# Narrow transpose of the softmax sums moved ahead of a cast, and the seventh pair's reciprocals sent through DRAM

## The chip, the core and the metric

The kernel runs on one core of a Trainium2 chip. The metric is the device time of one execution in microseconds (us), as the median of a few runs. The engines are TensorE (PE: matmuls and transposes into PSUM; PEld is its weight load), VectorE (DVE), ScalarE (ACT), GpSimd (POOL) and SyncE (SP, which here issues DMAs only). Each engine works through its own instructions in order; semaphores hold an instruction until what it needs from another engine or a DMA is there.

## The reference, cut to what matters

```python
# q, k, v: (2, 8, 768, 64); proj: (64, 6)
q_bucket = sum((q @ proj > 0) * powers); k_bucket = sum((k @ proj > 0) * powers)
scores = where(q_bucket == k_bucket, q @ k.T / 8, -1e9)
scores = scores - max(scores)
attn = exp(scores)
attn = attn / (sum(attn) + 1e-9)          # the row sums and their reciprocals
x = (attn @ v), heads side by side        # (1536, 512)
x = maximum(x @ w_in, 0) ** 2 @ w_out     # first MoE block, 512 -> 2048 -> 512
h = x @ w_in2
out = (h * sigmoid(h)) @ w_out2           # second MoE block
```

## The kernel before

There are 16 heads of 768 rows, worked off as 8 pairs of heads (`p` = 0 to 7). A pair has four units `u` (two heads, two halves of 384 query rows each), so there are 32 units, and each unit has six key tiles of 128. After attention the two MoE blocks follow in one long stretch whose order a planner sets (class `Plan`); the change does not touch it.

Attention is one hand-written loop over steps `d` (L1258). A step handles two key tiles, `g = 2d` and `g+1`. On PE a step is: six transposes of exponentials into two PSUM banks of the pool `ps_t` (`transp`, L1025, three per bank), four products of values with tiles that are two steps old (`av`, L1049 and L1050), and four score matmuls for a later tile (`score_mm`, L989). Every product is made of a high and a low part: ScalarE casts each transposed bank to the high part `th` (`t_hi`, L1030), and VectorE subtracts it from the bank to get the low part `tl` (`t_lo`, L1036). VectorE also takes the row maximum (L996), and ScalarE the exponential (`score_exp`, L1009), which adds up the row sums into `sums[p]`. A finished unit is copied by ScalarE (`ob`, L1060), and two DMAs on SP's queue move its two halves to `ta` and `tb`; POOL adds them up (`x_sum`, L1103). There are two `ta` buffers and one `tb`.

In the steps 5, 17, 29, 41, 53, 65 and 77 (here: **long steps**) PE also forms the hash bits of the next pair by twelve matmuls (`bits_mm`, L789), which VectorE compares (`bits_cmp`, L795, two of them). Two DMAs on SP's queue (`place_bits`, L919) put the bit rows into the `qq` and `kk` tiles, which the score matmuls read two steps later. VectorE has some word operations of the MoE weights in these steps too (L958, L962, L966).

The sums of pair `p` become reciprocals at step `d0+2`, where `d0 = 12(p+1)` (`norm_rows`, L1071). They must be laid out along the columns of `x`. This is done in three ways:

- Pairs 0 to 5, at the long steps 17 to 77: a **narrow transpose** on PE (`row_turn`, L1077: 128 sums x 12 into 12 rows at the end of the bank of tile `g+1`), a copy by ScalarE (L1079), a DMA into a DRAM scratch (`row_put`, L1083), and two DMAs back that repeat each row over 64 partitions (`row_get`, L1088). Then POOL multiplies `x` by it (`x_mul`, L1115) and splits blocks for the MoE (`x_put`, L1124 and L1125).
- Pair 6: POOL spreads the reciprocals (L1074), PE transposes them with six 128x128 transposes at step 93 (`rb_mm`, L1097) into a bank pair of `ps_s`, ScalarE copies the result (`x_norm`, L1108), and POOL multiplies.
- Pair 7: POOL spreads them too; after the loop PE transposes them (L1315) and VectorE multiplies (L1317).

What an engine does in a step stands in the order in which the Python calls it. `at(d, f, ...)` puts a call into the list `todo` of a step, run at its end. The narrow transpose stands behind `t_hi(g+1)`:

```python
                transp(g + 1)
                t_hi(g + 1)
                if d in turn:
                    row_turn(turn[d], PT[g + 1][0])
```

Of the kernel before, what the change touches and what calls it, by code (L numbers as in the profile page):

```python
# [11 lines left out]
F32 = mybir.dt.float32  # L12
# [5 lines left out]
ALU = mybir.AluOpType  # L18
# [6 lines left out]
NPAIR = B * H // 2  # L25
NU = NPAIR * 4
QW = 384
# [672 lines left out]
def lsh_attention_moe_moe(ctx, tc, kd, qk, qf, fq, v, pc, wi1, wo1, wi2, wo2, out):  # L700
    nc = tc.nc
# [19 lines left out]
    ps_s = att.enter_context(tc.tile_pool(name="ps_s", bufs=2, space=PSUM))  # L721
# [3 lines left out]
    ident = ac.tile([128, 128], F32, name="ident")  # L725
# [30 lines left out]
    def scale_q(p):  # L756
        q = pair[p]["r"][0]
        nc.scalar.mul(out=q, in_=q, mul=SCALE)
# [217 lines left out]
    P, stats, otile, sums = {}, {}, {}, {}  # L976

    def warm_up(n):
        for _ in range(n):
            mm(warm, zb[:, 0:128], zb[:, 0:512], start=True, stop=True)  # L980
# [13 lines left out]
    def row_max(u, j, s):  # L994
        m = mt[:, (u * 3 + j) % 4]
        nc.vector.tensor_reduce(out=m[:, 0:1], in_=s[:, :, 0:QW], op=ALU.max, axis=AX.XY, negate=True)  # L996
        return m

    def row_live(m):
        nc.vector.tensor_scalar(out=m[:, 1:2], in0=m[:, 0:1], scalar1=LIM, scalar2=1.0, op0=ALU.is_lt, op1=ALU.mult)  # L1000
        nc.vector.tensor_scalar(out=m[:, 2:3], in0=m[:, 0:1], scalar1=LIM, scalar2=m[:, 0:1], op0=ALU.is_lt, op1=ALU.mult)  # L1001

    def score_exp(u, j, s, m):
        p = u // 4
        if u % 4 == 0 and j == 0:
            sums[p] = a2.tile([128, 12], F32, tag="sums", name=f"sums{p}")
        e = P[u, j] = ac.tile([128, S], F32, tag="P", bufs=6, name=f"P{u}_{j}")
        c = (u % 4) * 3 + j
        nc.scalar.activation(  # L1009
            out=e.rearrange("p (a b) -> p a b", a=2),  # L1010
            in_=s[:, :, 0:QW],
            func=AF.Exp,
            scale=m[:, 1:2],
            bias=m[:, 2:3],
            accum_out=sums[p][:, c : c + 1],
        )

    PT = {}

    def transp(g, t=None):  # L1020
        u, kt = divmod(g, KT)
        if t is None:
            t = ps_t.tile([128, 512], F32, tag="t", name=f"t{g}")
        for j in range(3):
            nc.tensor.transpose(t[:, j * 128 : (j + 1) * 128], P[u, j][:, kt * 128 : (kt + 1) * 128], ident)  # L1025
        PT[g] = (t,)

    def t_hi(g):
        th = a1.tile([128, QW], F32R, tag="th", bufs=6, name=f"th{g}")
        nc.scalar.copy(out=th, in_=PT[g][0][:, 0:QW])  # L1030
        PT[g] += (th,)

    def t_lo(g):
        t, th = PT[g]
        tl = a1.tile([128, QW], F32R, tag="tl", bufs=6, name=f"tl{g}")
        nc.vector.tensor_tensor(out=tl, in0=t[:, 0:QW], in1=th.bitcast(F32), op=ALU.subtract)  # L1036
        PT[g] = th, tl

    xs = {}
# [29 lines left out]
    def norm_rows(p):  # L1069
        ri = sums[p]  # L1070
        nc.vector.reciprocal(out=ri, in_=ri)  # L1071
        if p >= NPAIR - 2:
            w = rows[p] = a1.tile([128, 6, 2, 64], F32, tag="rw", bufs=2, name=f"rw{p}")
            nc.gpsimd.tensor_copy(out=w, in_=ri.rearrange("p (h c) -> p c h", h=2).unsqueeze(3).broadcast_to([128, 6, 2, 64]))  # L1074

    def row_turn(p, t):
        nc.tensor.transpose(t[0:12, QW:512], sums[p], ident)  # L1077
        r = turned[p] = a1.tile([12, 128], F32, tag="rt", name=f"rt{p}")
        nc.scalar.copy(out=r, in_=t[0:12, QW:512])  # L1079

# [9 lines left out]
    turned, scratch = {}, {}  # L1090
    rows = {}

    def rb_mm(p):
        s = ps_s.tile([128, 2, 512], F32, tag="s", name=f"rb{p}")
        for c in range(6):
            o = s[:, c // 3, c % 3 * 128 : c % 3 * 128 + 128]
            nc.tensor.transpose(o, rows[p][:, c].rearrange("p h d -> p (h d)"), ident)  # L1097
        return s

    def x_sum(p):  # L1100
        ta, tb = xs[p]
        for r, z in ((slice(0, 64), slice(QW, S)), (slice(0, 128), slice(0, QW))) if p == NPAIR - 1 else ((slice(0, 128), slice(0, S)),):
            nc.gpsimd.tensor_tensor(out=ta[r, z], in0=ta[r, z], in1=tb[r, z], op=ALU.add)  # L1103

    def x_norm(s, p):
        ta = xs[p][0].rearrange("p (a b) -> p a b", a=2)
        if p < NPAIR - 1:
            nc.scalar.copy(out=rows[p].rearrange("p c h d -> p (c h d)").rearrange("p (a b) -> p a b", a=2), in_=s[:, :, 0:QW])  # L1108
        else:
            nc.vector.tensor_tensor(out=x_rows(p).rearrange("p (a b) -> p a b", a=2), in0=s[:, :, 0:QW], in1=ta, op=ALU.mult)  # L1110

    def x_mul(p):
        if p < NPAIR - 1:
# [3 lines left out]
    def x_rows(p):  # L1117
        return yf[:, p % 4, p // 4 * S : p // 4 * S + S]
# [11 lines left out]
        nc.gpsimd.tensor_tensor(out=o, in0=o, in1=b, op=ALU.subtract if MINUS[0].get(k) else ALU.add)  # L1130

    todo = defaultdict(list)
    extra = defaultdict(list)
    mid = defaultdict(list)
    long, scale, turn = {}, {}, {}
    last = defaultdict(list)

    def at(g, fn, *a):
        todo[g].append((fn, a))

    for p in range(1, NPAIR):
        d0 = 12 * (p - 1)
# [18 lines left out]
    for p in range(NPAIR):  # L1161
        d0 = 12 * (p + 1)
        at(d0 + (-3 if p < NPAIR - 1 else -4), norm_sums, p)
        at(d0 + (2 if p < NPAIR - 1 else -3), norm_rows, p)
        at(d0 + (3 if p < NPAIR - 1 else 0), x_sum, p)
        if p == NPAIR - 2:
            extra[d0 + 9].append((rb_mm, x_norm, p))
            at(d0 + 10, x_mul, p)
            at(d0 + 10, x_put, p)
        elif p < NPAIR - 2:  # L1170
            k = d0 + 5
            turn[k] = p
            at(k, row_put, p)
            at(k + 3, row_get, p)
            at(k + 5, x_mul, p)
            at(k + 5, x_put, p)

    for k, d in enumerate(X_STEPS):
        at(d, x_form, k)
    for i, (d_load, d_abs, *d_dve) in enumerate(W_STEPS):  # L1180
# [6 lines left out]
        d0 = d_dve[2]  # L1187
# [6 lines left out]
    with tc.manual_schedule():  # L1194
# [15 lines left out]
        c, k = slice(64, 64 + NBR), first["c"]  # L1210
        nc.vector.tensor_tensor(
            out=pdx, in0=k[:, 0:NBR].unsqueeze(1).broadcast_to([128, 2, NBR]), in1=k[:, NBR : 3 * NBR].rearrange("p (a b) -> p a b", a=2), op=ALU.mult
# [45 lines left out]
        for d in range(-5, G // 2 + 3):  # L1258
            ready, new = new, None
            g = 2 * d  # L1260
            if ready:
                m = row_max(*ready)
            if 0 <= g - 1 < G and g - 1 not in early_lo:
                t_lo(g - 1)
            if ready:
                row_live(m)
            for fn, a in mid.pop(d, []):
                fn(*a)
            if 0 <= g < G and d in (92, 94):
                t = ps_s.tile([128, 2, 512], F32, tag="s", name=f"t{g}")  # L1270
                for i in range(2):
                    transp(g + i, t[:, i])
                t_hi(g)
                t_hi(g + 1)
                t_lo(g)
            elif 0 <= g < G:
                transp(g)
                t_hi(g)
                t_lo(g)
                transp(g + 1)  # L1280
                t_hi(g + 1)
                if d in turn:
                    row_turn(turn[d], PT[g + 1][0])
            more = extra.pop(d, [])
            if ready and more and d not in long:
                score_exp(*ready, m)
            if d in long:
                score_exp(*ready, m)
                if d in scale:
                    scale_q(scale.pop(d))  # L1290
            for n in (g - V_LAG, g + 1 - V_LAG):
                if 0 <= n < G:
                    av(n)
            if d in long:
                t = bits_mm(long[d])
            held = [(dve, pe(p), p) for pe, dve, p in more]
            if d in long:
                bits_cmp(t, long[d], 0)
                t_lo(g + 1)
                bits_cmp(t, long[d], 1)  # L1300
            for dve, t, p in held:
                dve(t, p)
            if ready and not more and d not in long:
                score_exp(*ready, m)
            u, j = divmod(d + 5, 3)
            if u < NU:
                new = u, j, score_mm(u, j)
            for fn, a in todo.pop(d, []) + last.pop(d, []):
                fn(*a)
            warm_up(WARM.get(d, 0))  # L1310
        p = NPAIR - 1
        for z in (1, 0):
            t = ps_t.tile([128, 512], F32, tag="t", name=f"rb{p}_{z}")
            for j in range(3):
                nc.tensor.transpose(t[:, j * 128 : (j + 1) * 128], rows[p][:, 3 * z + j].rearrange("p h d -> p (h d)"), ident)  # L1315
            ta = xs[p][0][:, z * QW : (z + 1) * QW]
            nc.vector.tensor_tensor(out=x_rows(p)[:, z * QW : (z + 1) * QW], in0=t[:, 0:QW], in1=ta, op=ALU.mult)  # L1317
        assert not new
        assert not todo and not extra and not mid and not scale
        att.close()  # L1320


# [3 lines left out]
        t = dict(yf=yf, xk=xk, wpa=wpa, raw=raws, wt=wt, pair=both, src=((wi1, wo1), (wi2, wo2)), out=out)  # L1326
# [58 lines left out]
```

## Time and profile before

| | us |
|---|---|
| median of 3 runs | 729.46 (729.27 to 729.68) |
| profiled execution | 728.33 |
| its span (first to last instruction) | 726.6 |
| PE busy | 714.7 (98%) |
| DVE busy | 610.8 (84%) |
| ACT busy | 539.7 (74%) |
| POOL busy | 258.7 (36%) |

All times below are us from the start of the span. Attention takes the first 235 us or so, the MoE blocks the rest. A timeline row gives the start, the duration, the engine, the line, what is written from what, how often, and in brackets how long the engine was idle before and what ended that. Neighbouring instructions overlap in the pipeline, so a duration is longer than the distance to the next start. The chain of waits follows the work that ended last back to the start and says on which engine each piece of the span was.

### The profile page before, as it was taken

What the parts mean: (1) busy time and instruction counts of PE and PEld (TensorE: products, weight loads), DVE (VectorE), ACT (ScalarE), POOL (GpSimd) and SP (SyncE); (2) the same over time, 40 slices, a digit from 0 to 9 for tenths busy, and PEclk for the clock granted to TensorE, in tenths of its full rate; (3) what the DMA queues carried; (4) which work ended last, traced back from release to release, by engine and by line L of the source; (5) the groups of instructions that cost most, each with busy time, mean ns of one, the idle gap of its engine ahead of it and who ended that gap; (6) DMA issues with size and microseconds to landing.
All of it is one profiled execution on the core that took longest, in us unless ns stands there. A gap on an engine that the chain in (4) does not pass through costs nothing.

```text
span 726.6 us, 10910 instructions
## 1 busy us (share of the span) xinstructions
PE 714.7 (98%) x3643; PEld 612.2 (84%) x3643; DVE 610.8 (84%) x1106; ACT 539.7 (74%) x1012; POOL 258.7 (36%) x242
## 2 busy tenths in 40 slices
PE   8999999999999999999999999999999999999998
PEld 4999898898899888888888888888788888888886
DVE  7999999999998979786797879989778778888840
ACT  6998898898798898486459568878766945854861
POOL 7634755656547512041231223234203110212300
PEclk9999999999999999999999999999999999999999
DMA  5887698697662536124534653368231332345432
GB/s 172 202 199 169 158 204 187 153 222 175 147 157 55 122 107 169 59 73 102 130 88 116 133 134 96 87 143 172 70 124 58 88 89 80 107 102 116 102 110 93
DMA packets 38640, 92.16 MB, mean 127 GB/s; under 512 B 5564, under 2 KB 10524, under 8 KB 38584
## 3 DMA queue, kind: packets, MB, share of 16 engines
q1 hardware_dynamic: 26120, 67.18, 31.7%
q0 software_dynamic: 12032, 23.79, 18.3%
q8 instruction: 29, 0.48, 0.3%
q10 hardware_dynamic: 432, 0.49, 0.2%
q14 instruction: 27, 0.22, 0.1%
HBM read 51.96 MB, written 3.18 MB: 76 GB/s over the span
## 4 chain that ended last, share of the span: by engine, by line
PE 80%; DVE 15%; ACT 3%; issue 1%; DMA 0%; POOL 0%; ACTq 0%; DVEq 0%; POOLq 0%
PE bank L558 36%; PE bank L443 24%; DVE mt L996 7%; PE bank L420 7%; DVE tl L1036 6%; PE s L989 3%; PE t L1025 3%; PE o L1049 2%; PE o L1050 2%; ACT P L1009 2%; PE bs L789 1%; PE bt L789 1%; DVE mt L1001 1%; ACT th L1030 1%; DVE mt L1000 1%
## 5 line engine op out<-in xcount | busy, mean ns | idle before, releaser
L558 PE MATMUL bank<-woh,cell 128*128 128x512 f32 (+1 forms) x392 | 120.0, 385 | 0.0
L558 PE MATMUL bank<-cell,woh 128*128 128x512 f32 x384 | 118.3, 389 | 0.0
L1036 DVE TENSOR_TENSOR tl<-t,th 128x384 fp32r<-128x384 f32 x192 | 104.7, 548 | 0.8 <-ACT th L1030 0.8
L1009 ACT ACTIVATE P<-s,mt 128x768 f32<-128x768 f32 x96 | 95.3, 993 | 11.2 <-DVE mt L1001 8.1
L996 DVE TENSOR_REDUCE mt<-s 128x1 f32<-128x768 f32 x96 | 91.5, 953 | 3.5 <-PE s L989 3.1
L1030 ACT CAST th<-t 128x384 fp32r<-128x384 f32 x192 | 81.9, 483 | 12.5 <-PE t L1025 12.1
L558 PEld LDWEIGHTS bank<-woh,cell 128*128 128x128 f32 x392 | 73.1, 188 | 14.7
L558 PEld LDWEIGHTS bank<-cell,woh 128*128 128x128 f32 x384 | 72.1, 188 | 15.2
L989 PE MATMUL s<-kk,qq 76*128 76x384 f32 (+1 forms) x384 | 83.8, 339 | 0.5 <-ACT P L1009 0.4
L1025 PE MATMUL t<-ident,P 128*128 128x128 f32 x576 | 78.9, 272 | 0.0
L278 DVE TENSOR_TENSOR cell<-bank,cell 128x512 f32<-128x512 f32 x91 | 62.1, 692 | 18.3 <-PE bank L443 13.9
L443 PE MATMUL bank<-xw,wpb 128*128 128x512 f32 x312 | 75.9, 389 | 0.0
L558 PE MATMUL bank<-wol,cell 128*128 128x512 f32 (+1 forms) x196 | 75.4, 385 | 0.0
L558 PE MATMUL bank<-cell,wol 128*128 128x512 f32 x192 | 74.7, 389 | 0.0
L1049 PE MATMUL o<-th,vv 128*128 128x384 f32 x192 | 72.5, 377 | 0.0
L1025 PEld LDWEIGHTS t<-ident,P 128*128 128x128 f32 x576 | 67.8, 140 | 4.5 <-DVE tl L1036 0.2
L989 PEld LDWEIGHTS s<-kk,qq 76*128 76x128 f32 (+1 forms) x384 | 68.3, 188 | 2.6 <-ACT P L1009 1.6
L443 PEld LDWEIGHTS bank<-xw,wpb 128*128 128x128 f32 x312 | 58.5, 188 | 12.4 <-DVE bank L278 0.3
L1050 PE MATMUL o<-tl,vv 128*128 128x384 f32 x192 | 64.3, 335 | 0.0
L588 ACT COPY yf<-bank 128x512 f32<-128x512 f32 x48 | 27.9, 586 | 35.4 <-PE bank L558 34.7
L450 ACT COPY cell<-bank 128x512 f32<-128x512 f32 x39 | 22.9, 587 | 40.7 <-PE bank L443 38.7
L268 ACT CAST cell<-cell 128x512 fp32r<-128x512 f32 x81 | 48.8, 617 | 1.9 <-DMA cell<-cell 0.8
(201 smaller groups left out, 1484.8 us busy)
## 6 DMA issues: line engine op xcount, KB each, us to landing
raw<-in_dram SPq DMA_DIRECT2D x64, 512.0 KB
cell<-cell POOLq DMA_DIRECT2D x23, 256.0 KB, 3.4
qq<-hq SPq DMA_DIRECT2D x28, 192.0 KB
kk<-in_dram POOLq DMA_DIRECT2D x14, 384.0 KB, 5.3
yf<-cell POOLq DMA_DIRECT2D x21, 256.0 KB, 3.3
vr<-in_dram SPq DMA_DIRECT2D x8, 384.0 KB
ta<-ob SPq DMA_DIRECT2D x31, 96.0 KB
tb<-ob SPq DMA_DIRECT2D x31, 96.0 KB
```

What stands on the lines that cost most here:

```text
L278: add("DVE", 0.70, lambda: vec.tensor_tensor(out=val(out), in0=bank[b], in1=val(other), op=ALU.add), [("bank", b), *reads], writes)
L420: mm(bank[b], wpa[n][:, p, 4 * h + j], x[:, q], start=j == 0 and z == 0, stop=j == 3 and z == 2)
L443: mm(bank[b], w[:, p], x[:, q], start=not started and z == 0, stop=z == 2, skip_group_check=started)
L558: mm(bank[b][:, 0:wd], x, y, start=start and i == 0 and z == 0, stop=i == (FB if half is None else 2 * half + 2) - 1 and z == 2, skip_grou ...
L989: mm(s[:, n, 0:QW], t["qq"][h][0:kk, ab, c0 : c0 + 128], t["kk"][h][0:kk, ab, n * QW : (n + 1) * QW], start=ab == 0, stop=ab == 1)
L996: nc.vector.tensor_reduce(out=m[:, 0:1], in_=s[:, :, 0:QW], op=ALU.max, axis=AX.XY, negate=True)
L1009: nc.scalar.activation(out=e.rearrange("p (a b) -> p a b", a=2), in_=s[:, :, 0:QW], func=AF.Exp, scale=m[:, 1:2], bias=m[:, 2:3], accum_ou ...
L1025: nc.tensor.transpose(t[:, j * 128 : (j + 1) * 128], P[u, j][:, kt * 128 : (kt + 1) * 128], ident)
L1030: nc.scalar.copy(out=th, in_=PT[g][0][:, 0:QW])
L1036: nc.vector.tensor_tensor(out=tl, in0=t[:, 0:QW], in1=th.bitcast(F32), op=ALU.subtract)
L1049: mm(o[:, 0:QW], vv, th, start=kt == 0, stop=False)
L1050: mm(o[:, 0:QW], vv, tl, start=False, stop=kt == KT - 1)
```

## The change

The narrow transpose is issued by PE right behind the transposes of tile `g+1`, ahead of ScalarE's cast of that bank; ScalarE's copy of the 12 rows stays behind the cast. Pair 6 takes the way of pairs 0 to 5: narrow transpose at step 88 (not a long step), `row_put` at 88, `row_get` at 90, `x_mul` at 93; its spread on POOL, the six transposes on PE and the 768-column copy on ScalarE go. For pairs 0 to 4 `x_mul` moves from `d0+10` to `d0+13` and `x_put` to `d0+14`. Pair 5 keeps its steps.

```diff
-        if p >= NPAIR - 2:
+        if p == NPAIR - 1:
             w = rows[p] = a1.tile([128, 6, 2, 64], F32, tag="rw", bufs=2, name=f"rw{p}")
...
-    def row_turn(p, t):
-        nc.tensor.transpose(t[0:12, QW:512], sums[p], ident)
+    def row_copy(p, t):
         r = turned[p] = a1.tile([12, 128], F32, tag="rt", name=f"rt{p}")
         nc.scalar.copy(out=r, in_=t[0:12, QW:512])
...
-        if p == NPAIR - 2:
-            extra[d0 + 9].append((rb_mm, x_norm, p))
-            at(d0 + 10, x_mul, p)
-            at(d0 + 10, x_put, p)
-        elif p < NPAIR - 2:
-            k = d0 + 5
+        if p < NPAIR - 1:
+            k = d0 + (5 if p < NPAIR - 2 else 4)
             turn[k] = p
             at(k, row_put, p)
-            at(k + 3, row_get, p)
-            at(k + 5, x_mul, p)
-            at(k + 5, x_put, p)
+            at(k + (3 if p < NPAIR - 2 else 2), row_get, p)
+            x = k + (8 if p < NPAIR - 3 else 5)
+            at(x, x_mul, p)
+            at(x + 1 if p < NPAIR - 3 else x, x_put, p)
...
                 transp(g + 1)
+                if d in turn:
+                    nc.tensor.transpose(PT[g + 1][0][0:12, QW:512], sums[turn[d]], ident)
                 t_hi(g + 1)
                 if d in turn:
-                    row_turn(turn[d], PT[g + 1][0])
+                    row_copy(turn[d], PT[g + 1][0])
```

On PE the order of the instructions around a narrow transpose is the same in both kernels; what each waits for is not. These are PE's rows of step 17 before (`t_885` is the bank of tile `g+1`, `sums` the reciprocals, `o` the output bank that the products with `th` and `tl` open; in brackets the engines whose semaphore an instruction waits for):

```order
L1025 MATMUL t_885<-ident,P_0_689 128x128 [waits DVE_49]
L1025 MATMUL t_885<-ident,P_1_723 128x128
L1025 MATMUL t_885<-ident,P_2_757 128x128
L1077 MATMUL t_885<-ident,sums_191 12x128 [waits Activation_49,Pool_49]
L1049 MATMUL o_897<-th_812,vv_479 128x384
L1050 MATMUL o_897<-tl_814,vv_479 128x384
```

The narrow transpose waits for ScalarE there. The same rows of the changed kernel:

```order
L1025 MATMUL t_885<-ident,P_0_689 128x128 [waits DVE_49]
L1025 MATMUL t_885<-ident,P_1_723 128x128
L1025 MATMUL t_885<-ident,P_2_757 128x128
L1263 MATMUL t_885<-ident,sums_191 12x128 [waits Pool_49]
L1049 MATMUL o_897<-th_812,vv_479 128x384 [waits Activation_49]
L1050 MATMUL o_897<-tl_814,vv_479 128x384
```

The wait for ScalarE now stands one instruction later, on the first product that opens a new output bank.

POOL's rows around the multiplication of pair 1 before (`lp` is the low part of the keys of a later pair, `kk` its key load, `rw` the reciprocals from DRAM):

```order
L754 CAST hk_930<-rk_698 128x768
L1115 TENSOR_TENSOR yf<-rw_1046,ta_415 128x768
L1124 CAST xk<-yf 128x512
L1125 TENSOR_TENSOR xk<-yf,xk 128x512
L774 TENSOR_TENSOR lp_1006<-rk_698,hk_930 128x768
L764 DMA kk_0_1218<-in_dram 64x2x768
L1103 TENSOR_TENSOR ta_857<-ta_857,tb_858 128x768
```

And in the changed kernel:

```order
L754 CAST hk_930<-rk_698 128x768
L774 TENSOR_TENSOR lp_1006<-rk_698,hk_930 128x768
L764 DMA kk_0_1215<-in_dram 64x2x768
L1100 TENSOR_TENSOR yf<-rw_1046,ta_415 128x768
L1109 CAST xk<-yf 128x512
L1110 TENSOR_TENSOR xk<-yf,xk 128x512
L1095 TENSOR_TENSOR ta_857<-ta_857,tb_858 128x768
```

The three instructions that wait for the reciprocals now stand behind the split of the keys and the key load, still ahead of `x_sum`.

POOL's rows at the end of attention before, from pair 6's spread on (`rw_3505` and `sums_2845` are pair 6's, `rw_3719` and `sums_3288` pair 7's; `ta_3122` is pair 6's `x`, `ta_3562` pair 7's):

```order
L1074 COPY rw_3505<-sums_2845 128x768
L1103 TENSOR_TENSOR ta_3122<-ta_3122,tb_3123 128x768
L1130 TENSOR_TENSOR yf<-yf 128x512 x2
L1067 TENSOR_SCALAR sums_3288<-sums_3288 128x2x2
L1067 TENSOR_SCALAR sums_3288<-sums_3288 128x2x4
L1074 COPY rw_3719<-sums_3288 128x768
L1115 TENSOR_TENSOR yf<-rw_3505,ta_3122 128x768
L1103 TENSOR_TENSOR ta_3562<-ta_3562,tb_3563 64x384
```

In the changed kernel (`rw_3640` is what comes back from DRAM for pair 6, `rw_3718` pair 7's spread):

```order
L1095 TENSOR_TENSOR ta_3122<-ta_3122,tb_3123 128x768
L1115 TENSOR_TENSOR yf<-yf 128x512 x2
L1067 TENSOR_SCALAR sums_3288<-sums_3288 128x2x2
L1067 TENSOR_SCALAR sums_3288<-sums_3288 128x2x4
L1100 TENSOR_TENSOR yf<-rw_3640,ta_3122 128x768
L1074 COPY rw_3718<-sums_3288 128x768
L1095 TENSOR_TENSOR ta_3563<-ta_3563,tb_3564 64x384
```

Pair 6's multiplication now stands ahead of pair 7's spread and not behind it, and it waits for a DMA. On SP's queue pair 6's three new DMAs stand behind the first `ta` and `tb` transfers of pair 7.

## Rows read from the trace of the kernel before

**Rows 1.** Busy time of the engines, and the chain's share by engine.

```profile
PE 714.7 (98%) x3643; PEld 612.2 (84%) x3643; DVE 610.8 (84%) x1106; ACT 539.7 (74%) x1012; POOL 258.7 (36%) x242
PE 80%; DVE 15%; ACT 3%; issue 1%; DMA 0%; POOL 0%; ACTq 0%; DVEq 0%; POOLq 0%
```

**Rows 2.** Timeline of PE in step 5, a long step without a narrow transpose.

```profile
25.86 0.82 PE L1025 MATMUL t<-ident,P 128*128 128x128 f32 x6
26.44 0.42 PE L1049 MATMUL o<-th,vv 128*128 128x384 f32 x1
```

**Rows 3.** Timeline of PE in step 17 and the scores two steps later.

```profile
52.64 0.82 PE L1025 MATMUL t<-ident,P 128*128 128x128 f32 x6
54.50 0.27 PE L1077 MATMUL t<-ident,sums 128*12 128x128 f32 x1 [1.04 <-ACT th L1030]
54.53 0.42 PE L1049 MATMUL o<-th,vv 128*128 128x384 f32 x1
...
61.54 0.87 PE L989 MATMUL s<-kk,qq 128*128 128x384 f32 x4
```

**Rows 4.** Timeline of ScalarE in step 17.

```profile
53.50 0.86 ACT L1030 CAST th<-t 128x384 fp32r<-128x384 f32 x2
...
54.97 0.98 ACT L1009 ACTIVATE P<-s,mt 128x768 f32<-128x768 f32 x1
```

**Rows 5.** Groups by line: busy us, mean ns of one, idle before and its releaser.

```profile
L1077 PE MATMUL t<-ident,sums 128*12 128x128 f32 x6 | 1.6, 269 | 6.2 <-ACT th L1030 6.2
L795 DVE TENSOR_SCALAR bt<-bs,tmt 48x384 fp32r<-48x384 f32 x7 | 4.7, 667 | 4.0 <-PE bs L789 4.0
L1115 POOL TENSOR_TENSOR yf<-rw,ta 128x768 f32<-128x768 f32 x7 | 12.9, 1842 | 41.2 <-DMA rw<-rows 41.2
```

**Rows 6.** Timeline of VectorE in steps 17 to 19.

```profile
54.82 0.69 DVE L962 SCALAR_TENSOR_TENSOR wi<-raw,wi 128x512 uint32<-128x512 uint32 x1
...
56.56 0.67 DVE L795 TENSOR_SCALAR bt<-bs,tmt 48x384 fp32r<-48x384 f32 x1 [0.58 <-PE bs L789]
...
57.61 0.66 DVE L795 TENSOR_SCALAR bt<-bt,tmt 48x384 fp32r<-48x384 f32 x1
...
60.38 0.96 DVE L996 TENSOR_REDUCE mt<-s 128x1 f32<-128x768 f32 x1 [0.34 <-PE s L989]
```

**Rows 7.** Timeline of SP's queue behind the long step 77.

```profile
199.91 0.77 SPq L919 DMA_DIRECT2D kk<-bt  x1
```

**Rows 8.** Timeline of PE, the scores two steps behind step 77.

```profile
202.07 0.86 PE L989 MATMUL s<-kk,qq 128*128 128x384 f32 x4
```

**Rows 9.** Timeline of VectorE in step 77.

```profile
194.90 1.70 DVE L966 SCALAR_TENSOR_TENSOR both<-raw,both 128x512 uint32<-128x512 uint32 x1
```

**Rows 10.** Timeline of POOL from step 60 to the end of attention.

```profile
159.16 1.84 POOL L1115 TENSOR_TENSOR yf<-rw,ta 128x768 f32<-128x768 f32 x1 [7.75 <-DMA rw<-rows]
...
194.20 1.84 POOL L1103 TENSOR_TENSOR ta<-ta,tb 128x768 f32<-128x768 f32 x1
...
222.48 1.84 POOL L1103 TENSOR_TENSOR ta<-ta,tb 128x768 f32<-128x768 f32 x1
...
231.48 0.82 POOL L1074 COPY rw<-sums 128x768 f32<-128x768 f32 x1 [2.69 <-DVE sums L1071]
...
235.28 1.02 POOL L1103 TENSOR_TENSOR ta<-ta,tb 128x384 f32<-128x384 f32 x1 [0.19 <-DMA tb<-ob]
```

**Rows 11.** Timeline of SP's queue, the same stretch.

```profile
152.42 1.16 SPq L1088 DMA_DIRECT2D rw<-rows  x2
...
233.05 0.60 SPq L1062 DMA_DIRECT2D tb<-ob  x1
```

**Rows 12.** Timeline of PE at the end of attention.

```profile
234.50 0.82 PE L1315 MATMUL rb<-ident,rw 128*128 128x128 f32 x6
```

**Rows 13.** Timeline of VectorE at the end of attention.

```profile
231.33 0.50 DVE L1036 TENSOR_TENSOR tl<-t,th 128x384 fp32r<-128x384 f32 x1
232.17 1.95 DVE L1036 TENSOR_TENSOR tl<-t,th 128x384 fp32r<-128x384 f32 x4 [0.34 <-ACT th L1030]
```

More of the change, by code (lines that the diff above doesn't have):

```diff
@@ L1091, in lsh_attention_moe_moe @@
     rows = {}
[L1093 to L1098, printed above, removed]
     def x_sum(p):
@@ L1103, in x_sum @@
             nc.gpsimd.tensor_tensor(out=ta[r, z], in0=ta[r, z], in1=tb[r, z], op=ALU.add)
[L1105 to L1110, printed above, removed]
     def x_mul(p):
@@ L1132, in lsh_attention_moe_moe @@
     todo = defaultdict(list)
-    extra = defaultdict(list)
     mid = defaultdict(list)
@@ L1280, in lsh_attention_moe_moe @@
                 transp(g + 1)
+                if d in turn:
+                    nc.tensor.transpose(PT[g + 1][0][0:12, QW:512], sums[turn[d]], ident)
                 t_hi(g + 1)
                 if d in turn:
-                    row_turn(turn[d], PT[g + 1][0])
-            more = extra.pop(d, [])
-            if ready and more and d not in long:
-                score_exp(*ready, m)
+                    row_copy(turn[d], PT[g + 1][0])
             if d in long:
@@ L1295, in lsh_attention_moe_moe @@
                 t = bits_mm(long[d])
-            held = [(dve, pe(p), p) for pe, dve, p in more]
             if d in long:
@@ L1300, in lsh_attention_moe_moe @@
                 bits_cmp(t, long[d], 1)
-            for dve, t, p in held:
-                dve(t, p)
-            if ready and not more and d not in long:
+            if ready and d not in long:
                 score_exp(*ready, m)
@@ L1318, in lsh_attention_moe_moe @@
         assert not new
-        assert not todo and not extra and not mid and not scale
+        assert not todo and not mid and not scale
         att.close()
```

## Prediction

> **What bounds the kernel now.** I read the busy line and the chain first [rows 1]. PE is busy for 98% of the span and carries 80% of the chain, and the MoE blocks that follow attention run on PE without a gap, so what PE saves in attention comes off the end one for one. VectorE carries 15% of the chain, all in attention: the question is whether PE or VectorE paces the steps there.
>
> The second view is PE's timeline of two long steps. In step 5, without a narrow transpose, the first product with `th` starts 26.44 - 25.86 = 0.58 us after the first of the six transposes [rows 2]. In step 17 it is 54.53 - 52.64 = 1.89, and the row between shows why: the narrow transpose found PE idle for 1.04, until ScalarE's cast [rows 3]. ScalarE started its two casts only at 53.50 and was done at 54.36 [rows 4]. The grouped rows say that this is no accident of one step: six narrow transposes, 6.2 us idle before them, all of it for the cast, and 1.6 busy [rows 5]. VectorE in its turn waited for PE's bits, 4.0 in all over seven long steps [rows 5]. So in these steps PE is late, and VectorE behind it.
>
> **The narrow transpose ahead of the cast.** Idle and own time of the six are 6.2 + 1.6 = 7.8 us; step 17 against step 5 gives the same, 1.89 - 0.58 = 1.31 apiece. Issued straight behind the other transposes, one costs the distance between two of them: six last 0.82, the last alone 0.27 [rows 2, 3], so (0.82 - 0.27)/5 = 0.11. There are now seven, 0.77 in all. 7.8 - 0.77 = **7.0 us** less on PE, 1.20 in each of the six steps less the seventh's 0.11.
>
> What is late next? In step 17 PE would start the products at 52.64 + 0.58 + 0.11 = 53.33. The first of them now carries a wait for ScalarE of its own: it opens a new output bank, which ScalarE's copy of the old one must have emptied. ScalarE runs in order and that copy and the exponential behind it stand ahead of the casts, so both were over by 53.50 [rows 4]; the bits, four products later than 53.33, find their bank free. ScalarE's copy of the 12 rows no longer waits, so the next exponential starts soon after 54.36 and not at 54.97 [rows 4], ahead of the scores that need its bank. Both PE's and ScalarE's own waits are then gone.
>
> VectorE gains less. It has 0.58 idle ahead of the first compare, so with word operations ahead of it [rows 6] it can be only 0.58 earlier where PE is 1.20 earlier. It then lags by 0.62, and gets this back two steps later, where it was idle for 0.34, and in what small gaps follow [rows 6]. PE does not wait for its compares except through the bit rows: the second compare ends at 57.61 + 0.66 - 0.58 = 57.69, two DMAs on SP put the bits into `qq` and `kk`, and the second half of the scores two steps on, at 61.54 + 0.43 - 1.20 = 60.77, reads them. The DMA to `kk` stands behind the one to `qq`, whose issue I take as long as its own 0.77 [rows 7]; with 0.1 around it, it is issued at 58.6, which leaves 2.2. The tightest pass in the trace is step 77: issue at 199.91 [rows 7], second half of the scores at 202.07 + 0.43 = 202.50 [rows 8], 2.6 us with no stall. The nearest DMA whose landing shows took 235.28 - 233.05 = 2.2 from issue [rows 10, 11], or 1.6 behind the end of its 0.60 issue; with the 0.77 of a `kk` issue [rows 7] that second reading gives 2.4. So PE waits 0 to 0.3 here. Four of the six steps (17, 29, 53, 77) have two word operations ahead of the compare. Bounds 0 and 4 x 0.3 = 1.2; I take **0.3**, nearer the landing read from issue.
>
> **Pair 6.** PE loses six 128x128 transposes, at 0.11 each 0.66. Not all of it reaches the end: the last products need VectorE's last five subtractions. ScalarE's 768-column copy goes, so the casts come earlier and the 0.34 idle between [rows 13] closes: five in a row from 231.33 at (1.95 - 0.55)/3 = 0.47, the last ending at 231.33 + 4 x 0.47 + 0.55 = 233.76 and not 232.17 + 1.95 = 234.12. Bounds 0.36 and 0.66; I take **0.5**.
>
> What it adds is a way through DRAM with POOL and SP behind it. `row_put` stands on SP behind the `tb` transfer, which waits for `x_sum` of pair 6; that ended at 222.48 + 1.84 = 224.32 [rows 10] and comes 0.8 earlier without the spread ahead of it, 223.5. One issue of 0.6, then the put: about 224.1. No row shows a put alone; by the `tb` transfer's 2.2 it lands at 226.3, the two gets are issued by 226.3 + 1.16 = 227.5 [rows 11]. They land 2.2 (the `tb` transfer) to 5.6 later (from 152.42 + 1.16 to 159.16, where a 384 KB load stood behind them [rows 10, 11]), so `x_mul` starts between 229.7 and 233.1. Behind it on POOL now stands pair 7's spread, on which PE waits after the last products: 1.84 + 0.82 [rows 10] puts its end between 232.4 and 235.8. PE asks for it at 234.50 - 0.5 = 234.0 [rows 12]. Cost 0 to 1.8; I take 0, since no large load is issued beside these transfers. ScalarE's narrow copy at step 88 (0.26) replaces 0.80 of copy later, and the reciprocals and VectorE are untouched.
>
> **The other steps for x.** POOL waited 41.2 us in six multiplications for the DMA from DRAM [rows 5], 7.75 in the longest [rows 10], with the split and load of the keys behind it. These now go first; the multiplication still starts when its data land. `x_sum` is behind it as before but no longer behind the split and the load, so it is over 2 us sooner. No matmul of PE in these steps waited for POOL by the trace: I cost this at nothing. It could matter by way of VectorE: a word operation that takes 0.69 in step 17 [rows 6] took 1.70 in step 77 [rows 9], while POOL's `x_sum` ran from 194.20 to 196.04 [rows 10].
>
> The Trainium skill (SBUF — State Buffer, "Who interferes with whom") says that a VectorE instruction with two SBUF inputs and a GpSimd instruction that reads SBUF exclude each other for a whole instruction; the 1.70 beside the running `x_sum` agrees. By that rule work that POOL does at other times could block a word operation in a long step; the rival for it is the third below.
>
> **Sum.** 7.0 + 0.5 - 0.3 = 7.2 us. The profiled execution took 728.33, so 721.1; the median of the runs is 1.13 above that execution, so **722.3 us** against 729.46.
>
> **Rivals.**
> - *VectorE paces attention* (chance 0.10). Then only its own idle time comes off: 4.0 less the 0.34 or so of step 5, with 0.4 at the end: 4.1, so 725.4 us. For it: 15% of the chain [rows 1]. Against it: it still waits for PE's scores two steps after each long step [rows 6].
> - *Pair 6's data land late* (0.08): the 1.8 above, 7.2 - 1.8 = 5.4, so 724.1 us.
> - *POOL's moved work meets the word operations* (0.05). One blocked operation costs VectorE 1.70 - 0.69 = 1.0 and brings its lag in that step to 1.6; the bit rows then come about 1.0 late for PE. In two of the six steps 2.0 is given back: 724.3 us.
> - *The change doesn't do what it says* (0.04). If the wait that moved to the first product is for the cast after all, PE stands as long as before: 729 us, no change. Against it: that product's bank has nothing to do with the cast.
> - *Slower* (0.03), by one mechanism: POOL stuck in pair 6's multiplication. `x_mul` must start by 234.0 - 2.66 = 231.3 to cost nothing; from there each us of a late landing is a us of PE. It eats the whole 7.2 if `x_mul` starts at 238.5, so if the gets land 11.0 us after issue (227.5), twice the 5.6 seen; at 13.0 the kernel takes 731.5.
>
> **Chances and range.** The forecast holds 0.70. A difference under 0.2% (1.5 us) is about what a measurement of this kernel cannot tell from no change. Faster by more: 0.70 + 0.10 + 0.08 + 0.05 = 0.93; same 0.04; slower 0.03. The best case leaves the narrow transposes at no cost and the full 0.66: 7.8 + 0.66 = 8.5, so 721.0, and 0.2 for the spread of the runs: 720.8. Upward the forecast's own costs at their worst (7.0 + 0.36 - 1.2 - 1.8 = 4.4) give 725.1, and the first rival 725.4. Range 720.8 to 725.4.
>
> **What would show it.** In the profile of the changed kernel the group of narrow transposes has seven instructions and no idle time for the cast, the long steps with one last 0.11 more than step 5, and VectorE's idle time ahead of the first compare shrinks below 4.0. PE idle at scores behind a DMA would be the bit rows. At the end of attention PE reaches pair 7's transposes some 7.2 earlier, with no idle for POOL; idle there is the second rival. I am wrong if PE's saved time turns up as new idle two steps after the long steps, or if the steps between lengthen past PE's own work.

## The result, and the profile after

The changed kernel takes **723.39 us** (median of 4 runs, 722.89 to 723.48) against 729.37 for the kernel before beside it: a ratio of 0.9917, with a 95% interval of 0.9900 to 0.9934. It is faster by 6.0 us; the forecast was 722.3 in a range of 720.8 to 725.4. The profiled execution took 722.89 us, its span is 721.1.

The busy line and the chain's share by engine, as in [rows 1]:

```profile
PE 715.0 (99%) x3637; PEld 611.6 (85%) x3638; DVE 608.8 (84%) x1106; ACT 538.7 (75%) x1012; POOL 258.0 (36%) x241
PE 95%; POOL 2%; DMA 1%; issue 1%; ACT 0%; DVE 0%; SPq 0%; POOLq 0%; ACTq 0%; DVEq 0%
```

VectorE's 15% of the chain are gone. The groups of [rows 5] now:

```profile
L1263 PE MATMUL t<-ident,sums 128*12 128x128 f32 x7 | 1.9, 273 | 0.0
...
L795 DVE TENSOR_SCALAR bt<-bs,tmt 48x384 fp32r<-48x384 f32 x7 | 4.6, 661 | 0.3 <-PE bs L789 0.3
...
L1100 POOL TENSOR_TENSOR yf<-rw,ta 128x768 f32<-128x768 f32 x7 | 13.3, 1895 | 13.4 <-DMA rw<-rows 13.3
```

The narrow transpose waits for nothing, VectorE's first compare waits for PE only in the one long step without a narrow transpose (0.3 where it was 4.0), and POOL waits 13.4 us for rows from DRAM instead of 41.2. The timeline of PE in step 17 and at the scores two steps on, against [rows 3]:

```profile
52.94 0.82 PE L1025 MATMUL t<-ident,P 128*128 128x128 f32 x6
53.60 0.27 PE L1263 MATMUL t<-ident,sums 128*12 128x128 f32 x1
53.62 0.42 PE L1049 MATMUL o<-th,vv 128*128 128x384 f32 x1
...
60.68 1.03 PE L989 MATMUL s<-kk,qq 128*128 128x384 f32 x4
```

The first product comes 53.62 - 52.94 = 0.68 behind the transposes, 1.89 before. But the scores last 1.03, and 0.87 in [rows 3]: their second half waits for the bit rows. The timeline of the weight loads (PEld) names the DMA:

```profile
61.09 0.30 PEld L989 LDWEIGHTS s<-kk,qq 76*128 76x128 f32 x2 [0.22 <-DMA kk<-bt]
```

The pitch from the first transposes of one step to the next shows it everywhere. Each of the six long steps went from 5.47 to 4.27 or so, 7.16 in all; the step that holds those scores went from 2.05 or so to 2.27, 2.18, 2.16, 2.22, 2.14 and 2.17, together 0.8 more.

The end of attention has a wait that was not there before. These are the timelines of POOL, ScalarE, VectorE and PE:

```profile
226.41 0.81 POOL L1074 COPY rw<-sums 128x768 f32<-128x768 f32 x1
227.19 1.01 POOL L1095 TENSOR_TENSOR ta<-ta,tb 64x384 f32<-64x384 f32 x1
...
228.21 0.47 ACT L1056 COPY ta<-o 64x384 f32<-64x384 f32 x1 [1.74 <-POOL ta L1095]
...
228.71 0.56 DVE L1057 TENSOR_TENSOR ta<-o,ta 64x384 f32<-64x384 f32 x1 [1.09 <-ACT ta L1056]
...
227.96 0.82 PE L1292 MATMUL rb<-ident,rw 128*128 128x128 f32 x6
229.33 12.56 PE L420 MATMUL bank<-xk,wpa 128*128 128x512 f32 x54 [0.55 <-DVE ta L1057]
```

PE's pair 7 transposes come 234.50 - 227.96 = 6.54 earlier than in [rows 12]. The first MoE product (L420) stood 0.57 behind them before, at 235.07, and stands 1.37 behind them now: 0.8 lost, waiting for VectorE's read of the last unit's output `o`. That read (L1057) did not come later against these transposes: it ended 229.27 - 227.96 = 1.31 behind their start here and 1.26 before, when the first MoE product did not wait for it:

```profile
235.20 0.56 DVE L1057 TENSOR_TENSOR ta<-o,ta 64x384 f32<-64x384 f32 x1 [1.08 <-ACT ta L1056]
```

### The profile page after: what moved, and what is told of

Read it like the earlier page. It is cut to its first block, busy times and chain, and to the rows that moved or that the text cites. A ratio compares the mean times of both kernels' runs of the same rounds, so it can differ in the third digit from the quotient of the medians.

```text
span 721.1 us, 10898 instructions
## 1 busy us (share of the span) xinstructions
PE 715.0 (99%) x3637; PEld 611.6 (85%) x3638; DVE 608.8 (84%) x1106; ACT 538.7 (75%) x1012; POOL 258.0 (36%) x241
## 4 chain that ended last, share of the span: by engine, by line
PE 95%; POOL 2%; DMA 1%; issue 1%; ACT 0%; DVE 0%; SPq 0%; POOLq 0%; ACTq 0%; DVEq 0%
PE bank L558 35%; PE bank L443 24%; PE s L989 9%; PE t L1025 9%; PE bank L420 7%; PE o L1049 5%; PE o L1050 4%; PE bs L789 1%; PE bt L789 1%; DMA cell<-cell 1%; DMA fk<-in_dram 1%; POOL kk L867 0%; POOL vv L933 0%; POOL qq L868 0%; ACT P L1009 0%
```

## The experiments

Each was timed beside the kernel before. A ratio in brackets is against that, with its 95% interval. The changed kernel was timed twice, at 723.39 and 723.92; kernels that were not timed side by side and differ by no more than about that are compared by their traces.

### The parts one by one

**The narrow transpose alone.** The kernel before, with the edit below, where `row_turn` keeps the copy of the rows alone.

```diff
                 transp(g + 1)
+                if d in turn:
+                    nc.tensor.transpose(PT[g + 1][0][0:12, QW:512], sums[turn[d]], ident)
                 t_hi(g + 1)
                 if d in turn:
                     row_turn(turn[d], PT[g + 1][0])
```

> The kernel before with the narrow transpose issued ahead of ScalarE's second cast, and nothing else: pair 6 stays on the row spread and the PE transposes, the steps for x stay where they were. Theory (the narrow transposes alone make both the gain and the new waits two steps after each long step): six long steps 1.20 us shorter, -7.2; the scores two steps later wait for the bit rows as in the changed kernel, +0.8; the first MoE product follows pair 7's transposes at 0.57 us as before. Sum -6.4: about 723.0 us against 729.4. Rival 1 (the waits two steps later come from the moved steps for x): no such waits, -7.2, about 722.2 us. Rival 2 (VectorE paces attention once PE is quicker): the steps between the long ones are longer than 2.055 us as well.

Measured: 725.94 us, from 723.73 to 730.7 (0.9960, 0.9943 to 0.9976). None of the three: nearly half of the expected 6.4 stayed out. The long steps before step 65 are 4.27 as expected, the bit rows are waited for behind them, and the first MoE product follows at 0.57; but around step 65 PE stands still twice. The timelines of POOL, VectorE and PE there:

```profile
156.97 1.84 POOL L1114 TENSOR_TENSOR yf<-rw,ta 128x768 f32<-128x768 f32 x1 [9.04 <-DMA rw<-rows]
...
160.81 1.84 POOL L774 TENSOR_TENSOR lp<-rk,hk 128x768 fp32r<-128x768 f32 x1
...
163.27 1.87 POOL L1102 TENSOR_TENSOR ta<-ta,tb 128x768 f32<-128x768 f32 x1
...
163.58 2.11 DVE L962 SCALAR_TENSOR_TENSOR both<-raw,both 128x512 uint32<-128x512 uint32 x1
...
167.35 0.52 PE L1025 MATMUL t<-ident,P 128*128 128x128 f32 x3 [0.59 <-DVE tl L1036]
...
171.70 0.59 PE L989 MATMUL s<-kk,qq 76*128 76x384 f32 x2 [0.63 <-DMA qq<-bt]
```

The multiplication of x waited 9.04 us for its rows, with the keys' split, the keys' load and the sum of `ta` and `tb` behind it in POOL's order. I first put the loss down to the late split (`lp`). The row of VectorE says otherwise: the word operation L962 lasts 2.11, where it lasts 0.69 in [rows 6]. It began at 163.58 while POOL's sum ran, and ended 0.55 behind the sum's end at 165.14. The two compares and the bit rows are behind it on VectorE. One execution is profiled, at 725.24; what takes single ones to 730.7 is not shown.

**The steps for x alone.** The kernel before, with

```diff
-            at(k + 5, x_mul, p)
-            at(k + 5, x_put, p)
+            x = k + (8 if p < NPAIR - 3 else 5)
+            at(x, x_mul, p)
+            at(x + 1 if p < NPAIR - 3 else x, x_put, p)
```

> The kernel before with the multiplications of x of pairs 0 to 4 at their new steps, behind the split and the load of the keys on POOL; nothing else altered. Theory (the moved steps only pay once PE is 7 us quicker and the keys' split would come too late): 729.4 us as before, within 0.3. Rival (they are worth their 2.5 to 3 us in any case): 726.5 to 727 us. Third way (they cost something by themselves, as x is late for what reads it): 730 us or more.

Measured: 729.10 us (0.9995, 0.9987 to 1.0004). No effect. While PE waits in every long step, a VectorE that is blocked there costs nothing: L962 took 1.42 in step 65 here and the compares ended on time, and the slow row of [rows 9] had cost nothing either.

**All but the steps for x.** The changed kernel, with the diff above turned round.

> The changed kernel with the multiplications of x of pairs 0 to 4 back at the steps they had before (five steps after the rows were turned, not eight); the narrow transpose stays ahead of the cast and pair 6 on its way through DRAM. Theory (POOL waits in the multiplication for the rows from DRAM, with the split of the next keys behind it on POOL and the keys' and bits' transfers behind that on SP; where the rows land late, PE waits in turn): as in the kernel with the narrow transposes alone, some 2 to 3 us slower than the changed kernel, 725.5 to 726.5 us, with a wide spread, and a wait of PE in or behind the long step at 65. Rival (that kernel lost its 2.5 us by pair 6's old way): 723.4 us as the changed kernel, and no such wait.

Measured: 726.60 us, from 725.17 to 729.17 (0.9961, 0.9947 to 0.9975), 2.7 slower than the changed kernel run beside it (next entry). So these steps, worth nothing alone, hold 2.7 us of the gain. Two of VectorE's rows in the long steps 41 and 65, and the same operation of step 65 in the changed kernel behind them:

```profile
109.25 1.98 DVE L962 SCALAR_TENSOR_TENSOR wi<-raw,wi 128x512 uint32<-128x512 uint32 x1
...
164.50 2.02 DVE L962 SCALAR_TENSOR_TENSOR both<-raw,both 128x512 uint32<-128x512 uint32 x1
```

```profile
162.82 0.68 DVE L962 SCALAR_TENSOR_TENSOR both<-raw,both 128x512 uint32<-128x512 uint32 x1
```

In the changed kernel POOL's sum ran from 160.64 to 162.47 and was over by then.

**The changed kernel once more.**

> The changed kernel once more, unaltered, beside the runs that it is compared with here. Expected about 723.4 us, and a first MoE product at 1.37 us behind pair 7's transposes in the profile. The waits for the bit rows two steps after the long steps, 0.08 to 0.21 us in the first profile, are expected again if they belong to the schedule; where one of them differs by more than 0.1, the landing of the DMA varies from one execution to the next.

Measured: 723.92 us, 723.06 to 724.75 (0.9923, 0.9911 to 0.9934), with the first MoE product at 1.37 as before. The wait behind step 17 was larger. The rows of SP, PE and PEld, of this run and then SP's of the first profile:

```profile
58.65 1.23 SPq L919 DMA_DIRECT2D kk<-bt  x1
...
61.45 0.62 PE L989 MATMUL s<-kk,qq 76*128 76x384 f32 x2 [0.38 <-DVE tl L1036]
...
61.45 0.30 PEld L989 LDWEIGHTS s<-kk,qq 76*128 76x128 f32 x2 [0.70 <-DMA kk<-bt]
```

```profile
58.76 0.76 SPq L919 DMA_DIRECT2D kk<-bt  x1
```

The same DMA of the same program took 1.23 to issue and not 0.76, and the step grew by that 0.47, from 2.27 to 2.74. Behind step 65 it is the same: 1.42 to issue and not 1.06, and a step of 2.51 and not 2.14. (PE's row names VectorE, one of whose subtractions ended at that moment; the weight load waits for the bit rows alone.)

**Pair 6 alone.** The changed kernel with x at its old steps and

```diff
-                if d in turn:
+                if d in turn and d not in long:
                     nc.tensor.transpose(PT[g + 1][0][0:12, QW:512], sums[turn[d]], ident)
                 t_hi(g + 1)
+                if d in turn and d in long:
+                    nc.tensor.transpose(PT[g + 1][0][0:12, QW:512], sums[turn[d]], ident)
```

> Pair 6's reciprocals through DRAM alone: the six narrow transposes of the long steps stand behind the cast as before, only pair 6's (step 88, not a long step) stands ahead of it; the multiplications of pairs 0 to 5 stay at the steps they had. Theory (the edit gives 0.7 us of PE in step 93, pays 0.1 for the narrow transpose, and pays 0.8 at the first MoE product, because one tile less in the score pool leaves the last unit's output in the bank that MoE opens first): +0.2 us, about 729.6 against 729.4, with a wait of PE for VectorE's read of that output ahead of the first MoE product. Rival (that wait of 0.8 comes because the whole end of attention is earlier than POOL's sums, and not from the banks): PE's end of attention is only 0.6 us earlier here, so the wait is at most 0.1 and the edit gains: -0.5, about 728.9.

Measured: 729.79 us (1.0007, 0.9999 to 1.0016), where the theory had 729.6. PE waits 0.56 ahead of the first MoE product, which again stands 1.37 behind pair 7's transposes, though attention is no earlier here than before:

```profile
235.53 0.82 PE L1293 MATMUL rb<-ident,rw 128*128 128x128 f32 x6
236.90 3.47 PE L420 MATMUL bank<-xk,wpa 128*128 128x512 f32 x14 [0.56 <-DVE ta L1057]
```

So the wait does not hang on how early PE comes; the bank is tried next. (This profile also lost 0.7 behind the steps 41 and 65, where `kk` took 1.24 and 1.61 to issue.)

### The two waits that the change left

**The bank.** The changed kernel, with

```diff
-    idle = [2, 3, 4, 7, 0, 1, 5, 6]
+    idle = [0, 1, 4, 7, 2, 3, 5, 6]
```

> The changed kernel with one constant altered: the order in which MoE opens its eight PSUM banks begins with the other pair of score banks, [0, 1, 4, 7, 2, 3, 5, 6] in place of [2, 3, 4, 7, 0, 1, 5, 6]. Theory (the bank holds the first MoE product up): the product follows pair 7's transposes at 0.57 us and not 1.37, so -0.8 against the changed kernel, about 722.6 us, if the banks opened next are free as well. Rival (the product waits for its data, or the wait moves to the next product behind pair 7's sums): under -0.2, about 723.3 us, with the idle time further on among the first MoE products.

Measured: 722.68 us (0.9908, 0.9894 to 0.9922). PE at the end of attention:

```profile
229.13 0.82 PE L1292 MATMUL rb<-ident,rw 128*128 128x128 f32 x6
229.70 12.51 PE L420 MATMUL bank<-xk,wpa 128*128 128x512 f32 x54
```

0.57 apart and no wait: the 0.8 is back. The pool `ps_s` deals out two bank pairs in turn. With pair 6's tile gone from it, the last unit's output lands in the other pair, the one that MoE opens first.

This run also shows that the moved steps for x do not rule the blocked word operation out. Its attention is the changed kernel's, but in step 65 POOL's sum came 1.4 later, behind a late `tb` transfer, and L962 met it. The rows of POOL and VectorE:

```profile
162.00 1.84 POOL L1095 TENSOR_TENSOR ta<-ta,tb 128x768 f32<-128x768 f32 x1 [1.79 <-DMA tb<-ob]
...
163.00 1.40 DVE L962 SCALAR_TENSOR_TENSOR both<-raw,both 128x512 uint32<-128x512 uint32 x1
```

The two steps behind took 2.25 and 2.93, and 2.07 and 2.14 in the first profile of the changed kernel.

**The bit rows.** The changed kernel, with

```diff
                 bits_cmp(t, long[d], 0)
-                t_lo(g + 1)
                 bits_cmp(t, long[d], 1)
+                t_lo(g + 1)
```

> The changed kernel with VectorE's two compares of the bits side by side in each long step; the subtraction that stood between them comes behind. The second compare starts about 0.46 us earlier, and with it the two DMAs of the bit rows. Theory (PE's scores two steps after the long steps wait for the bit rows' DMA): the six waits of 0.08 to 0.21 us, 0.8 in all, go: about -0.8, 722.6 us against 723.4. Rival 1 (VectorE, busy for 99% of these stretches, paces the steps): nothing is gained, 723.4 us, and the step pitch stays up. Rival 2 (the subtraction that now comes later holds a transposing bank, and PE waits for that in the next step): slower than the changed kernel by up to 0.4 us in each long step.

Measured: 722.30 us (0.9906, 0.9893 to 0.9918). The steps behind 17, 29, 41, 53 and 77 went back to 2.11, 2.05, 2.05, 2.05 and 2.05. The `kk` transfer behind step 17 is issued 0.28 earlier on the clock of the profile, 0.45 counted from the first transposes (16.35 here, 16.17 in the changed kernel), and the scores last 0.86 again:

```profile
58.48 0.82 SPq L919 DMA_DIRECT2D kk<-bt  x1
...
60.86 0.86 PE L989 MATMUL s<-kk,qq 128*128 128x384 f32 x4
```

So the bit rows were the wait, and VectorE does not set the pace there by itself. Behind step 65 this execution waited 0.39 even so, at 169.35: its `kk` transfer took 1.66 to issue.

**Both.** The changed kernel with the two edits.

> The changed kernel with both alterations: MoE opens the other score banks first, and VectorE's two compares of the bits stand side by side. Theory (two separate waits of PE, both on the path): the gains add, 0.7 for the bank and 0.7 to 1.1 for the bit rows, so about 721.8 us. Rival (with the bit rows gone VectorE paces, or the end of attention waits for POOL's sums): as the better of the two alone, about 722.4 us.

Measured: 721.59 us, 721.06 to 722.16 (0.9890, 0.9876 to 0.9904), the fastest kernel here, 2.3 under the changed kernel timed beside it (723.92). The gains add, and PE's only idle time named in attention is 0.2 at the start.

**Pair 6 with its bank wait out of the way.** The same, but pair 6 as before the change; the banks then rotate as before and keep their order.

> The narrow transposes ahead of the cast, the moved steps for x and the two compares side by side, but pair 6 as it was before: the row spread on POOL, six transposes on PE in step 93, the copy on ScalarE; the score banks then rotate as before and MoE opens its banks in its old order. Beside it stands the kernel with both alterations, 721.6 us, which differs by pair 6 and the order of the banks. Theory (with its bank wait out of the way pair 6's path through DRAM is worth its 0.7 us of PE in step 93 less 0.1 for its narrow transpose): 722.2 us. Rival (its transfers cost elsewhere what it saves): 721.6 us or less.

Measured: 722.56 us (0.9909, 0.9896 to 0.9923). The two kernels were not timed side by side, and the intervals overlap; the traces tell more. From the first transposes to the first MoE product PE takes 228.68 - 16.41 = 212.27 us here and 228.34 - 16.52 = 211.82 with pair 6 through DRAM: 0.45 less. Of that 0.06 is the wait behind step 65, which is not pair 6's (2.25 here, 2.19 there), so its new way is worth about 0.4, the narrow transpose of step 88 included.

**The load of v behind the bit rows.** The kernel with both edits, and

```diff
-        at(d0 + 5, load_v, p)
+        at(d0 + 6, load_v, p)
```

> The kernel with both alterations, and the load of v of the next pair (384 KB) one step later, so that SP issues it behind the bit rows and not ahead of them. Theory (the 0.4 to 0.6 us that PE waited for the bit rows behind step 65 in three of the profiles come from that load standing ahead of them in the queues): that wait goes, and the kernel is 0.2 to 0.5 us quicker than with both alterations alone, 721.3 to 721.6 us. Rival (the wait has another cause, and POOL, whose split of v stands two steps later, now waits for the load): equal or slower, 721.8 to 723 us.

Measured: 723.52 us (0.9915, 0.9902 to 0.9928), 1.9 slower. The theory fell: behind step 65 PE waited 0.38 with the load behind the bit rows too, and the `kk` transfer again took long to issue (1.64). POOL now waited 4.3 us in four steps for the load, and the second head's bit rows, which go out behind it, left SP at 150.05 and not at 147.62; PE waited 0.71 for them. In step 41 L962 took 1.68 beside POOL's sum, and the step behind lasted 2.60. POOL's wait for the load:

```profile
POOL vv L932 <- DMA vr<-in_dram: 4.3, 4, 1.9
```

### What the steps for x are worth, and why

**Word operations out of the way.** The kernel with x at its old steps, with the sign operation (L962) of two weight blocks moved:

```diff
-W_STEPS = (..., (8, 17, 29, 41, 53), (30, 41, 53, 65, 77), ...)
+W_STEPS = (..., (8, 17, 29, 35, 53), (30, 41, 53, 59, 77), ...)
```

> The kernel that has the multiplications of x at their old steps (726.6 us), with VectorE's sign operations of the MoE weights (L962) of two weight blocks taken out of the long steps 41 and 65 and put at steps 35 and 59, where POOL stands idle in its wait for the rows from DRAM. Its trace showed those operations taking 1.98 and 2.02 us beside POOL's sum of ta and tb, against 0.69 elsewhere. New theory (the late sum on POOL blocks the word operation, VectorE's compare and the bit rows come 1.3 us late, and PE waits at its transposes and its scores): the operations take 0.69 again, PE's waits in and behind steps 41 and 65 go, and the kernel gains 1.5 to 2.5 us: 724.1 to 725.1 us. Rival (the old theory: the split of the next keys comes too late on POOL, and SP's transfers behind it): POOL waits as before, and nothing is gained: 726.6 us.

Measured: 725.02 us, 724.46 to 727.41 (0.9940, 0.9927 to 0.9953), 1.6 under the kernel that it alters; the two were not timed side by side, and their intervals touch. POOL waits and splits the keys as late as before, but the steps behind 41 and 65, 2.84 and 2.88 in the kernel that it alters, are back at 2.07. So the late split is not the main cause. VectorE's operation in step 59, and the rows of VectorE, SP and PE further on:

```profile
151.24 0.68 DVE L962 SCALAR_TENSOR_TENSOR both<-raw,both 128x512 uint32<-128x512 uint32 x1
...
192.16 1.78 DVE L966 SCALAR_TENSOR_TENSOR both<-raw,both 128x512 uint32<-128x512 uint32 x1
...
165.72 0.76 SPq L928 DMA_DIRECT2D vr<-in_dram  x1
...
167.91 0.77 SPq L919 DMA_DIRECT2D kk<-bt  x1
...
171.52 0.59 PE L989 MATMUL s<-kk,qq 76*128 76x384 f32 x2 [0.84 <-DMA qq<-bt]
```

The moved operations take 0.68; one that was not moved, in step 77, is blocked in its turn (1.78). And PE still waits behind step 65, although `kk` is issued at 167.91 with no delay behind the compare: the scores go on 3.6 us later, 2.3 in step 17 of the changed kernel. There the load of v went out 1.3 us ahead of the bit rows, because the `tb` transfer ahead of it on SP had waited for POOL's late sum. That this load slows them is argued from one trace and was not tried in this kernel; in the kernel that issues it behind the bit rows (the entry above) the scores behind step 65 went on just as late, 3.2 after the issue of `kk`.

**The same in the fastest kernel.**

> The kernel with both alterations (721.6 us), with the same two sign operations at steps 35 and 59. Theory (bit rows of the steps behind 41 and 65 come up to 0.6 us earlier, since one word operation less stands ahead of the compares; PE hardly waited for them any more): what is left of the wait behind step 65 goes (0.15 in the profile), so 721.3 to 721.6 us, with a narrower spread. Rival (VectorE has no room for the operation in a short step, falls behind there by 0.6 and PE waits for it): 722 us or more.

Measured: 722.49 us (0.9903, 0.9890 to 0.9916), 0.9 over 721.59, not timed side by side and with intervals that overlap. PE's waits in attention:

```profile
PE t L1025 <- DVE tl L1036: 0.8, 2, 0.4
PE s L989 <- issue: 0.5, 1, 0.5
```

The two waits at the transposes come right behind steps 35 and 59: two steps there last 4.72 and 4.70 instead of 4.11. The third is behind step 65, where `kk` took 1.77 to issue. A short step has no room for 0.68 more on VectorE. The move cost the kernel of the entry above the same 1.2, so the two collisions that it took away were worth more than its 1.6.

## Why the prediction was right, and where it was off

- **The narrow transpose: right.** Forecast -7.0; the trace has 7.16 less in six long steps and 0.11 more in step 88, 7.05. The wait that moved to the first product cost nothing, and [rows 4] had been enough to see that.
- **The bit rows: right cause, wrong size.** Forecast 0.3 of bounds 0 to 1.2, measured 0.8. The landing was the mis-sized term: in step 17 `kk` was issued at 58.76, where the steps gave 58.6 (plus the 0.3 by which the whole profile starts later), but the weights of the second half went on only at 61.09, 2.33 behind that issue and 1.57 behind its end. I took the 2.2 of a transfer read from issue. The other reading of the same row, 1.6 behind the end of the issue, is what came: 1.57 to 1.64 in all six steps, two of which had a longer issue (1.10 in step 41, 1.06 in step 65). The wait also came in all six steps, not in four. The prediction's own sign of being wrong, new idle time two steps after the long steps, thus showed for 0.8 of the 7.
- **Pair 6: right.** Forecast -0.5; step 93 is 0.69 shorter, and the end behind it 0.25 longer (3.00 from the last transposes to pair 7's, 2.75 before), for the reason given: VectorE's last five subtractions. 0.44 from the two, without the 0.11 of step 88, which the first entry has; with it 0.33, and about 0.4 from the pair of kernels. Its rows landed in time: `x_mul` started at 224.23, and no transpose of PE waited for POOL.
- **What was missing: 0.8 at the first MoE product.** Pair 6 was costed by its time on PE, ScalarE and POOL, and not by the tile that it took from a rotating pool. The order of the changed program shows it without a run: the first MoE product carries a wait for VectorE there, and none before. So pair 6's edit as it stands gives back 0.8 where it gains 0.3 to 0.4.
- **The steps for x: costed at nothing, and for the wrong reason.** Alone they are worth nothing; with the narrow transpose they hold 2.7 us. The prediction knew the mechanism (the third rival, and the 1.70 of [rows 9]) but asked only whether POOL's *moved* work would meet VectorE's word operations. It was the unmoved work that would have met them, once PE was early enough for it to matter. That the 7.0 of the narrow transposes came out in full is luck in this part: by the prediction's sum a change without these steps would have taken the same time.
- **Rival 1, VectorE paces attention, did not come, but is near.** VectorE is busy 29.5 to 29.8 of every 30 us from 40 to 190 in the changed kernel, and 0.68 more in a short step is paid nearly in full.

The sum by the trace: -7.05 + 0.8 - 0.44 + 0.8 = -5.9, and from the first transposes to the first MoE product PE takes 213.16 instead of 219.20, -6.0. The medians differ by 6.0. (The two profiled spans differ by 5.5: the changed one has 0.3 more at the start, and 0.2 in MoE behind a DMA.)

## What to carry to other kernels

When a wait is taken off the engine that bounds, list what that wait had been hiding on the others, and price the parts of a change together: 3.3 us for one part, 0 for another and about -0.5 for the third (its interval just includes 0), each alone, made 6.0. A tile taken out of a pool shifts the rotation for every tile behind it, so look at what opens those banks next. A DMA's landing that is taken from the nearest row is better counted from the end of its issue, since the issue itself varies, and it belongs in the sum at the longer of its readings where the waiting engine has no slack left.

## What the runs showed of the hardware

Beside a POOL operation with two inputs in SBUF, a VectorE word operation with two inputs took 2.11, 1.98 and 2.02 us in place of 0.68, and ended 0.55 or 0.56 behind the POOL operation, which had begun 0.31 to 0.44 before it. It also goes the other way: in the changed kernel POOL's multiplication of pair 6 took 2.23 where it takes 1.84, beside VectorE's L966, which had begun 0.16 before it. The profile shows this as a longer operation, not as idle time. The Trainium skill (SBUF — State Buffer, "Who interferes with whom") calls the port pair that the two share an exclusive lock, and says that issue order decides which of them is blocked; these four rows agree. One pair of rows in the MoE blocks does not fit by its starts alone: in the changed kernel VectorE's L962 began at 238.60, 0.14 ahead of POOL's L261, and was the one that took long (2.32, ending 0.56 behind L261). A DMA issue of POOL was running there from 238.18, and why it came out so stays open.

I had not expected that the issue of one and the same 36 KB transfer on SP takes 0.76 us in one execution and 1.23 in the next, or 1.66 and 1.77 behind step 65 in other kernels, and that PE's scores come later by the difference. What lengthens it stays open. So does the landing behind step 65, which in some kernels was late without a long issue (3.6 us from an issue of 0.77 in the kernel with the moved word operations).
